# One list of places for all jobs, with the engine of each written down, in a planned attention and mixer kernel

## The chip, the cores and the metric

The kernel runs on one core of a Trainium2 chip. A core has TensorE (matmuls), VectorE, ScalarE, GpSimd (POOL in the rows), and SyncE, which here only issues DMAs. The metric is device time in microseconds (us) of one execution.

## The reference

Causal attention over 4 batches, 12 heads, 448 positions of width 64, then a mixer on the result `x` (448 x 768 in each batch), all in float32:

```python
scores = scale * np.matmul(q, k.transpose(0, 1, 3, 2))
scores = np.where(mask, -1000000000.0, scores)
attn = softmax(scores)                  # row maximum taken off, sum + 1e-09
x = np.matmul(attn, v)                  # heads side by side: 448 x 768
h = np.maximum(x.transpose(0, 2, 1) @ w_tok1, 0.0) @ w_tok2    # over positions
u = x + h.transpose(0, 2, 1)
out = u + np.maximum(u @ w_ch1, 0.0) @ w_ch2                   # over channels, 768 -> 1536 -> 768
```

(`softmax` stands for four lines of the reference.)

## The kernel before, in words

The heads are taken in pairs, 24 of them (`g`), six to a batch. For a pair: `load_pair` brings q, k and v; `prep` turns q and k on VectorE; `heads` does the scores on TensorE (`qk`, line 888, in two halves), takes row bounds on VectorE (`low`, line 910), exponentials with row sums on ScalarE (`expo`, line 922), then a small addition (`guard`, line 941) and a reciprocal (line 944). The probabilities are scaled (`norm`, through `copy`, lines 550 and 552) and transposed: the first ten pairs on TensorE (`by_tensor`, `flip`, line 979), the others by a transposing DMA on 16-bit halves (`by_dma`: `split`, DMA at line 1031, `merge`, through `words`, lines 556 and 558). `values` multiplies the result, the tile `pt`, with v (line 1075). `xturn` turns the result (line 1114) and splits it into a high and a low part, as every matmul of the mixer is done in three products of such parts. `tokens` does the two products over positions (lines 1162 and 1195), `split_u` splits the sum, `channels` and `group` do the products over channels (lines 1245, 1573, 1644, 1664), with weights that `narrow` and `parts` prepare: load, three steps on ScalarE and VectorE, a high part (`wh`) and the difference (`wl`, through `minus`, line 561). `store` and `finish` send the output. The weights of `tokens` have their own splits, in `token_weights` (`w1hi`, `w1lo`, `w2hi`, `w2lo`).

None of this is issued at once. Each step calls `plan.job`, with a planned cost for each engine that can do it, the jobs it needs, the buffers it holds and a rank. There are 2,335 jobs. `Plan.emit` then keeps a clock of its own and, whenever an engine is free on it, gives that engine the job of lowest rank among those whose needs are met and whose buffers are open. What it gives is the order of the program; an engine runs its instructions in that order. The rank of a job is that of its group (2.0 times the pair, and so on) plus a number from the table `NUDGE`, which has one number for all jobs of the same function and rank. Where several engines can do a job, the table `ONLY` names one for some groups, and for the rest a rule in `emit` decides (`BIAS`, `FIRST`, `EARLY`): the engine that takes the job must be the one that would end it first, with a handicap for each engine.

Where TensorE has no job on the planner's clock in the first 75 us and has been busy too little, `emit` issues `keep_warm` (line 778): a matmul of the mask tile by itself, 512 columns, whose result nobody reads.

Of the kernel before, what the change touches and what calls it, by code (L numbers as in the profile page):

```python
# [20 lines left out]
NUDGE = {  # L21
    "load_pair.blocks": {-2: -5.69, 0: -0.18, 2: 9.42, 4: 34.85, 6: 51.99, 8: 70.18, 10: 68.38, 12: -63.34,
        14: 307.44, 16: -211.48, 18: 1.58, 22: 59.15, 24: -9.93, 28: 0.02, 30: 485.43, 32: -30.92, 34: 1.04, 36: 2.18,
        38: -113.03, 40: 409.72, 42: 100.41, 44: -29.88},
    "load_pair.load": {0.5: 20.36, 2.5: -53.93, 4.5: 9.42, 6.5: 0.88, 8.5: 242.83, 10.5: 16.05, 12.5: 0.11,
        14.5: -63.34, 16.5: 0.03, 18.5: 31.27, 22.5: 29.43, 24.5: 16.6, 26.5: 117.07, 28.5: 0.11, 32.5: -0.55,
        34.5: 1.07, 38.5: 13.95, 40.5: 4.04, 42.5: -1.86, 44.5: 180.84, 46.5: -102.76},
    "load_pair.lower": {-0.2: -2.64, 3.8: -10.26, 5.8: -2.41, 7.8: 21.12, 9.8: 1.62, 13.8: 9.47, 15.8: -35.82,
        21.8: 29.43, 23.8: -9.31, 25.8: -12.47, 27.8: 0.13, 29.8: 31.38, 31.8: 31.04, 35.8: 27.32, 37.8: -7.85,
        39.8: 51.43, 41.8: -25.4, 45.8: 20.31},  # L30
    "load_pair.upper": {-0.2: -2.4, 1.8: 7.04, 3.8: 6.92, 5.8: -38.06, 9.8: -135.49, 11.8: -8.1, 13.8: -1.57,
        15.8: -37.81, 17.8: 12.16, 23.8: -89.08, 25.8: -67.22, 27.8: -3.95, 29.8: 7.11, 31.8: -0.97, 33.8: -6.33,
        37.8: -50.92, 39.8: -13.98, 41.8: 35.44, 43.8: 184.58, 45.8: 60.49},
    "narrow.load": {3.5: 36.16, 12: 184.21, 13: -0.75, 15: 1.63, 16: -155.64, 17: 80.6, 18: 1.18, 19: -3.98,
        21: -25.25, 22: -31.03, 23: 2.89, 24: -71.56, 25: -147.25, 27: 5.6, 28: -7.93, 29: -30.33, 30: -32.57,
        31: -0.15, 32: 17.21, 33: 66.76, 34: 41.75, 35: -91.73},
    "narrow.size": {3.5: -95.77, 13: -3.03, 14: 0.59, 15: 1.63, 17: 0.9, 18: -1.77, 19: -30.27, 21: -0.59, 22: 0.06,
        23: -32.71, 25: 30.04, 26: 14.77, 27: 6.97, 29: -25.08, 30: 0.04, 31: 69.05, 32: 0.35, 33: -0.72, 34: -12.68,
        35: -18.38},
    "narrow.shift": {3.5: -39.08, 12: -45.95, 13: -22.05, 14: 51.06, 15: -37.08, 16: 8.91, 17: 34.81, 18: 52.69,  # L40
        19: 16.31, 20: 19.85, 21: 6.15, 22: 148.69, 23: -16.03, 24: -33.15, 26: 110.05, 28: -6.86, 30: -0.29,
        31: -28.04, 32: -56.71, 33: 6.39, 34: -92.95, 35: 76.44},
    "narrow.join": {3.5: -34.13, 12: 72.73, 13: -67.18, 15: -0.22, 16: -15.64, 17: -42.91, 18: 337.03, 19: -32.99,
        20: -3.33, 21: -11.67, 22: -21.87, 23: 28.98, 24: -52.27, 25: -37.11, 26: -0.11, 28: 4.53, 30: -55.02,
        31: -18.66, 32: -38.67, 33: 0.07, 34: 172.82, 35: 92.85},
    "token_weights.<lambda>": {3.5: -7.44},
    "token_weights.rest_of": {3.5: 7.83},
    "prep.turn": {-1.5: 17.65, 2.5: -24.12, 4.5: 0.1, 6.5: -10.13, 8.5: -2.4, 12.5: -0.74, 14.5: 16.4, 18.5: 25.24,
        20.5: 64.35, 22.5: 76.68, 24.5: 54.69, 26.5: 13.64, 28.5: 13.68, 30.5: 5.63, 32.5: 1.14, 34.5: 19.37,
        36.5: 8.97, 38.5: -1.03, 40.5: 35.56, 42.5: 123.8, 44.5: -119.2},  # L50
    "heads.<lambda>": {0: -24.44, 2: -159.72, 4: -0.05, 6: 113.65, 8: 3.12, 10: 0.97, 12: 354.23, 14: -142.06,
        16: -43.97, 18: 52.02, 20: 87.45, 22: 61.7, 24: 12.81, 26: 1.2, 30: -2.24, 32: 122.48, 34: 141.23, 36: -10.17,
        38: 0.02, 40: 8.83, 42: -10.82, 44: 156.23},
    "heads.low": {0: 0.25, 2: 41.64, 6: -286.14, 8: -4.08, 10: -8.1, 12: 223.68, 14: 1016.35, 16: 767.17, 18: 134.37,
        20: 36.56, 24: 259.08, 26: -101.41, 28: 14.92, 30: 4.79, 34: 2.07, 36: 6.95, 38: -3.49, 40: 1.25, 42: -10.4,
        44: -155.06, 46: 25.76},
    "heads.expo": {0: 0.69, 2: 65.52, 4: 78.63, 6: 39.16, 8: 11.37, 10: 455.98, 12: 396.16, 14: -45.41, 16: -8.34,
        18: 134.37, 20: -16.55, 22: -10.41, 24: 203.57, 26: -86.73, 30: 12.87, 34: 2.07, 36: -25.22, 38: 1.67,
        40: -10.67, 42: 12.66, 44: -308.91, 46: 24.15},
    "heads.guard": {0: -45.33, 2: 1.89, 4: 10.39, 6: 0.51, 8: 33.2, 10: 499.55, 12: 379.6, 14: -1.91, 16: -8.27,  # L60
        18: -41.43, 20: -1.85, 22: -232.88, 24: -21.38, 26: -116.5, 28: 84.38, 34: -6.15, 36: 79.09, 38: 1.21,
        40: -0.86, 42: 9.74, 44: -41.52, 46: 9.28},
    "heads.recip": {0: 11.8, 4: 16.05, 6: 18.33, 8: -79.14, 10: -2.88, 12: 43.13, 16: -63.95, 18: -3.79, 20: -19,
        22: -0.44, 24: 164.82, 28: 36.75, 30: -0.68, 32: -4.73, 34: -3.56, 36: -1.87, 38: 75.88, 40: -0.8, 42: 6.81,
        44: 127.73, 46: 0.03},
    "by_tensor.norm": {0: 17.18, 2: 24.16, 6: 2.65, 8: -0.78, 10: -1.93, 12: -3.78, 14: -73.1, 18: 9.56},
    "values.pv": {0: 44.92, 2: -73.62, 6: -11.44, 8: -61.4, 10: -47.37, 12: -12.03, 14: 21.32, 16: -82.88,
        18: -106.29, 20: 59.59, 24: 4.27, 28: -0.09, 30: 0.7, 34: 0.08, 36: -43.42, 38: -13.99, 40: -1.77, 42: -4.13,
# [12 lines left out]
        41: -12.64, 43: -0.55, 45: -4.69},
    "by_tensor.flip": {2: 22.46, 4: -94.38, 6: -48.95, 8: -0.63, 10: 4.97, 12: -6.6, 14: 375.47, 16: -40.39, 18: 10},
    "xturn.twice": {1: -40.45, 5: -61.16, 9: 14.26, 17: 25.81, 21: 1.6, 25: -6.91, 29: 87.65, 33: 1.12, 37: 1.51,
        41: 68.8, 45: 1.15},
    "xturn.none": {1: -35.52, 5: -149.33, 9: -0.41, 13: 0.01, 17: 0.32, 21: -12.3, 25: 67.43, 29: -23.48, 33: -127.73,
        37: -16.01, 45: 11.99},
    "tokens.tok1": {4.5: -2.49, 8.5: 13.1, 12.5: 0.42, 16.5: -32.58, 20.5: -1.53, 24.5: -5.35, 32.5: -45.94,
        36.5: 7.23, 40.5: -1.94, 48.5: -18.08},
    "tokens.relu": {-5: -496.54},
    "tokens.lo": {-5: 26.43},  # L90
    "tokens.tok2": {4.5: 3.06, 8.5: -7.61, 12.5: 15.8, 16.5: 14.51, 20.5: -2.1, 24.5: -94.87, 28.5: -76.06,
        32.5: 562.97, 36.5: 0.62, 40.5: 1421.86, 48.5: 71.6},
# [66 lines left out]
    "finish.plus": {-6: 210.3},  # L159
    "finish.turn": {-6: -5.28},  # L160
    "finish.evac": {-6: -32.31},
    "finish.send": {-6: 0.08},
}


# [100 lines left out]
class Plan:  # L266
# [6 lines left out]
    SHARE = 0.0  # L273
# [1503 lines left out]
```

## Time and profile before

| | us |
|---|---|
| median of 3 runs | 556.01 (553.76 to 556.63) |
| the profiled execution | 554.26 |
| its span, first to last instruction | 552.5 |
| TensorE busy | 542.3 (98%) |
| VectorE busy | 438.0 (79%) |
| ScalarE busy | 338.8 (61%) |
| GpSimd busy | 123.3 (22%) |

The profile gives for each engine how long it ran instructions, and for each idle time what ended it. A busy TensorE is not one at its peak, since its matmuls overlap: a product of 448 columns is listed with some 366 ns, and six in a row take 1.22 us. PEclk is the share of the clock that was granted. All rows come from the profiled execution.

### The profile page before, as it was taken

How to read it: one execution, taken by the hardware profiler on the slowest of the kernel's cores; microseconds unless marked ns; L12 is line 12 of the kernel's file. 1: busy time of each engine (PE TensorE's matmuls, PEld its weight loads, DVE VectorE, ACT ScalarE, POOL GpSimd, SP SyncE). 2: the span in 40 equal slices, each digit the busy share in tenths (PEclk: the TensorE clock that was granted, in tenths of full speed). 3: DMA queues.
4: the chain of work that ended last, by engine and by line, in shares of the span. 5: the costliest groups of instructions: out<-in, count | busy, mean ns of one | idle time of the engine just before them, and what ended most of it. 6: DMA issues, size and time to landing. Idle time of an engine off the chain costs nothing.

```text
span 552.5 us, 11198 instructions
## 1 busy us (share of the span) xinstructions
PE 542.3 (98%) x3922; PEld 469.7 (85%) x3928; DVE 438.0 (79%) x1062; ACT 338.8 (61%) x780; POOL 123.3 (22%) x182
## 2 busy tenths in 40 slices
PE   8999999998999999999999999999999999999997
PEld 4678788886888988888888788899999999999996
DVE  5898888889897788698787887779998857584854
ACT  4989878898857995696796897663332313140401
POOL 2534461362235001030200210223100313100000
PEclk9999999999999999999999999999999999999999
DMA  6677766898998989989998957328551111111257
GB/s 113 155 153 153 168 153 183 195 185 118 204 211 191 171 191 225 193 152 221 190 190 152 208 149 150 95 84 167 117 122 57 58 57 59 57 58 57 58 71 130
DMA packets 231784, 77.69 MB, mean 141 GB/s; under 512 B 206000, under 2 KB 221232, under 8 KB 231728
## 3 DMA queue, kind: packets, MB, share of 16 engines
q1 hardware_dynamic: 220112, 75.37, 63.9%
q10 hardware_dynamic: 11616, 1.61, 1.8%
q8 instruction: 31, 0.51, 0.4%
q14 instruction: 25, 0.20, 0.2%
HBM read 49.15 MB, written 14.94 MB: 116 GB/s over the span
## 4 chain that ended last, share of the span: by engine, by line
PE 90%; DVE 3%; DMA 2%; SPq 2%; ACT 1%; issue 1%; ACTq 0%; POOL 0%; DVEq 0%
PE ps L1245 30%; PE ps L1664 15%; PE ps L1573 12%; PE ps L1075 7%; PE ps L888 7%; PE ps L1195 5%; PE ps L1162 5%; PE ps L979 3%; PE ps L1644 3%; PE ps L1114 2%; PE ps L778 1%; DMA wraw<-in_moe_w_ch_dram 1%; DMA out_dram<-kq 1%; SPq L806 1%; DVE pt L558 1%
## 5 line engine op out<-in xcount | busy, mean ns | idle before, releaser
L1312 DVE TENSOR_TENSOR u<-ps,u 128x448 f32<-128x448 f32 x118 | 72.7, 620 | 40.0 <-PE ps L1664 27.0
L922 ACT ACTIVATE prob<-prob,stat 128x256 f32<-128x256 f32 (+6 forms) x168 | 83.8, 501 | 20.2 <-DVE stat L910 19.4
L910 DVE CUSTOM_DVE_ANT_0 prob<-ps,mask 128x448 f32<-128x448 f32 (+6 forms) x168 | 63.8, 415 | 5.4 <-PE ps L888 5.1
L1245 PE MATMUL ps<-uh,wh 128*128 128x448 f32 x144 | 55.0, 382 | 0.0
L1245 PE MATMUL ps<-gh,wh 128*128 128x448 f32 x144 | 54.0, 375 | 0.0
L1245 PE MATMUL ps<-uh,wl 128*128 128x448 f32 x144 | 52.9, 367 | 0.2 <-DVE wl L561 0.2
L1245 PE MATMUL ps<-gh,wl 128*128 128x448 f32 x144 | 52.7, 366 | 0.0
L1245 PE MATMUL ps<-gl,wh 128*128 128x448 f32 x144 | 52.7, 366 | 0.0
L1245 PE MATMUL ps<-ul,wh 128*128 128x448 f32 x144 | 52.6, 365 | 0.0
L550 ACT ACTIVATE wh<-wf 128x768 fp32r<-128x768 f32 x32 | 26.8, 842 | 38.5 <-PE ps L1664 21.9
L888 PE MATMUL ps<-kq,kq 64*64 64x128 f32 (+5 forms) x768 | 46.6, 362 | 1.0 <-DVE stat L944 0.6
L552 POOL TENSOR_SCALAR prob<-prob,stat 128x64 f32<-128x64 f32 (+6 forms) x63 | 34.6, 565 | 44.0 <-DVE stat L944 39.1
L888 PEld LDWEIGHTS ps<-kq,kq 64*64 64x64 f32 x768 | 27.9, 132 | 19.3 <-issue 12.9
L556 ACT COPY prob<-prob 128x1024 uint16<-128x1024 uint16 (+1 forms) x45 | 41.5, 941 | 3.3 <-DVE prob L552 2.7
L1075 PE MATMUL ps<-pt,vraw 128*64 128x256 f32 (+2 forms) x480 | 39.7, 310 | 2.8 <-DVE pt L558 2.8
L1075 PEld LDWEIGHTS ps<-pt,vraw 128*64 128x64 f32 x480 | 29.0, 136 | 15.4 <-DVE pt L558 3.2
L561 DVE TENSOR_TENSOR wl<-wf,wh 128x768 fp32r<-128x768 f32 x36 | 35.7, 998 | 2.3 <-ACT wh L550 1.5
L556 ACT COPY pt<-pt 128x384 uint16<-128x384 uint16 (+3 forms) x42 | 33.5, 868 | 4.1 <-PE ps L888 3.0
L550 ACT ACTIVATE u<-wf 128x768 fp32r<-128x768 f32 (+1 forms) x17 | 12.7, 749 | 34.2 <-PE ps L1573 19.5
L922 ACT ACTIVATION_READ_ACCUMULATOR prob<-prob,stat 128x1 f32 x168 | 31.9, 190 | 0.0
L1664 PE MATMUL ps<-u,wh 128*128 128x448 f32 x108 | 30.7, 366 | 0.0
L1245 PEld LDWEIGHTS ps<-uh,wl 128*128 128x128 f32 x144 | 27.0, 188 | 3.2 <-DVE wl L561 1.0
(213 smaller groups left out, 1412.2 us busy)
## 6 DMA issues: line engine op xcount, KB each, us to landing
wraw<-in_moe_w_ch_dram SPq DMA_DIRECT2D x24, 768.0 KB, 5.6
wf<-scratch SPq DMA_DIRECT2D x30, 384.0 KB, 3.4
scratch<-wf SPq DMA_DIRECT2D x24, 384.0 KB, 3.4
vraw<-in_v_dram SPq DMA_DIRECT2D x48, 96.0 KB, 2.7
kq<-in_k_dram SPq DMA_DIRECT2D x60, 56.0 KB, 3.9
kq<-in_q_dram SPq DMA_DIRECT2D x56, 56.0 KB, 2.4
gh<-in_k_dram SPq DMA_DIRECT2D x36, 56.0 KB, 2.5
gl<-in_q_dram SPq DMA_DIRECT2D x36, 56.0 KB, 2.4
```

What stands on the lines that cost most here:

```text
L550: nc.scalar.activation(dst, src, AF.Copy, scale=scale)
L552: eng[e].tensor_scalar(dst, src, scale, 0.0, op0=ALU.mult, op1=ALU.add)
L556: nc.scalar.copy(out, in_)
L561: eng[e].tensor_tensor(dst, a, b, op=ALU.subtract)
L888: nc.tensor.matmul(scores[n].tile[lanes, to:at], lhsT=qe.tile[LANES[j], c * QC:(c + 1) * QC], rhs=ke.tile[LANES[j], slice(*keys)], start=T ...
L910: nc.vector.tensor_tensor_reduce(out=part(c, r), in0=ps.tile[:, at:at + wide(c)], in1=mask[:, S - QC:S + P] if c == 2 else mask[:, S - wid ...
L922: nc.scalar.activation(part(c, r), part(c, r), AF.Exp, bias=stat.tile[:, 0, AT[c]:AT[c] + 1], scale=-1.0, accum_out=stat.tile[:, 1, AT[c]: ...
L1075: nc.tensor.matmul(ps.tile[LANES[j], c * QC:(c + nq) * QC], lhsT=s.tile[:, kb, j] if kb < NCH else ends.tile[:, kb - NCH, j], rhs=view[:, ...
L1245: nc.tensor.matmul(ps.tile[:, :S], lhsT=x.tile[:, at_:at_ + P], rhs=y, start=(n == 0 and i == 0), stop=(n + 1 == w[2] and i == 2),)
L1312: eng[e].tensor_tensor(u, ps.tile[:, :S], u, op=ALU.add)
L1573: nc.tensor.matmul(ps.tile[:, :S], lhsT=l()[:, t * P:(t + 1) * P], rhs=r, start=(t == 0 and n == 0), stop=(t == half - 1 and n == 2),)
L1664: nc.tensor.matmul(ps.tile[:, :S], lhsT=l.tile[:, t * P:(t + 1) * P], rhs=r.tile, start=(n == 0), stop=(n == 3 * len(fs) - 1),)
```

## The change

`NUDGE` and `ONLY` go, and with them the rule that chose an engine. `PLACES` has a number from 0 to 2,334 for each job by itself (a tuple for each function and old rank, in the order in which the jobs are made), and `CHOICE` has a letter for each job that more than one engine can do: a for ScalarE, d for VectorE, p for GpSimd. The old rank is only the key into both. `emit` is otherwise as it was: needs, buffers, its clock and the warming matmuls. Two smaller edits come with it: in `QUARTERS` the two last pairs of score matmuls change places, and the planned costs of the two halves of the scores are new.

```diff
-NUDGE = {
-    "load_pair.blocks": {-2: -5.69, 0: -0.18, 2: 9.42, 4: 34.85, 6: 51.99, 8: 70.18, 10: 68.38, 12: -63.34,
...
+PLACES = {
+    "load_pair.blocks": {-2: (2, 3), 0: (4, 5), 2: (20, 10), 4: (52, 70), 6: (138, 160), 8: (213, 238), 10: (272,
...
-ONLY = {
-    "token_weights.<lambda>": {3.5: "act"},
-    "token_weights.rest_of": {3.5: "pool"},
...
+CHOICE = {
+    "token_weights.<lambda>": {3.5: "pppppppp"},
+    "token_weights.rest_of": {3.5: "ddppddpp"},
...
-    BIAS = {"act": 600.0, "dve": 4500.0, "pool": 6850.0}
-    FIRST = {"act": 425.0, "dve": 1000.0, "pool": 500.0}
-    EARLY = 50.0
-    SHARE = 0.0
...
-        only = ONLY.get(name, {}).get(round(rank, 3))
-        if only in costs:
+        key = name, round(rank, 3)
+        nth = self.seen[key] = self.seen.get(key, -1) + 1
+        if len(costs) > 1:
+            only = {"a": "act", "d": "dve", "p": "pool"}[CHOICE[name][key[1]][nth]]
             costs = {only: costs[only]}
-        rank = rank + NUDGE.get(name, {}).get(round(rank, 3), 0.0)
+        rank = PLACES[name][key[1]][nth]
...
-                    if open_ and len(j.costs) > 1:
-                        bias = self.BIAS if j.rank >= self.EARLY or j.rank < -4 else self.FIRST
-                        end = until(j, e, now) + bias[e]
-                        open_ = all(
-                            end <= until(j, o, max(free[o], now)) + self.SHARE * load[o] + bias[o]
-                            for o in j.costs if o != e
-                        )
...
-                (0, 2, 4), (1, 2, 4), (0, 3, 3), (1, 3, 3), (0, 3, 1), (1, 3, 1), (0, 2, 2), (1, 2, 2))
+                (0, 2, 4), (1, 2, 4), (0, 3, 3), (1, 3, 3), (0, 2, 2), (1, 2, 2), (0, 3, 1), (1, 3, 1))
...
-        for rg, cost in zip(RG, (825.0, 695.0)):
+        for rg, cost in zip(RG, (820.0, 850.0)):
```

Line numbers of the changed kernel are 83 higher from the planner's middle on (line 550 is 633, line 778 is 861, line 1114 is 1197, line 1162 is 1245).

What the lists do to the program is seen in the order of each engine's instructions. TensorE before, from the value products of the third pair to the second of eight warming matmuls that stand ahead of a transpose (`vend` is the end of v, `u` the result of the attention, `prob` the probabilities):

```order
144 L1075 MATMUL ps_529<-pt_424,vend_98 64x64 x6
145 L778 LDWEIGHTS mask
146 L778 MATMUL ps_87<-mask 128x512
...
149 L1114 MATMUL ps_577<-ident,u_369 128x128 x4
150 L778 LDWEIGHTS mask
151 L778 MATMUL ps_87<-mask 128x512
```

TensorE now, from the value products of the same pair to the first product over positions:

```order
144 L1158 MATMUL ps_551<-pt_450,vend_98 64x64 x6
145 L1062 MATMUL ps_593<-across_ident,prob_1_94 128x128 x4
146 L971 MATMUL ps_603<-kq_546,kq_588 64x448 x2
147 L971 MATMUL ps_604<-kq_546,kq_588 64x384 x2
...
155 L971 MATMUL ps_617<-kq_546,kq_588 64x128 x2
156 L1197 MATMUL ps_641<-ident,u_393 128x128 x4
157 L1062 MATMUL ps_650<-ident,prob_1_95 128x128 x3
158 L861 LDWEIGHTS mask
159 L861 MATMUL ps_87<-mask 128x512
160 L1245 MATMUL ps_659<-xh_478,w1hi 128x256
```

The scores of the fifth pair now stand where warming matmuls stood; one warming matmul is left there.

ScalarE before, around the first splits of the token weights (`stat` holds row sums, `wf` a weight before it is split):

```order
40 L610 ACTIVATE wf_492<-wl_418 128x256
41 L939 ACTIVATE stat_449<-stat_449 128x3
42 L550 ACTIVATE u_369<-ps_451 128x448
43 L550 ACTIVATE w1hi<-wf_474 128x256
44 L550 ACTIVATE w1hi<-wf_492 128x256
45 L610 ACTIVATE wf_535<-wh_435 128x256
46 L550 ACTIVATE xh_394<-ps_523 128x4x128
47 L922 ACTIVATE prob_1_94,stat_449<-prob_1_94,stat_449 128x320
```

ScalarE now, at the same place:

```order
44 L693 ACTIVATE wf_510<-wl_435 128x256
45 L1005 ACTIVATE prob_1_94,stat_423<-prob_1_94,stat_423 128x320
46 L1005 ACTIVATE prob_1_94,stat_423<-prob_1_94,stat_423 128x192
47 L633 ACTIVATE u_393<-ps_469 128x448
48 L1022 ACTIVATE stat_423<-stat_423 128x4
49 L633 ACTIVATE pt_450<-ps_516 128x3x128
50 L693 ACTIVATE wf_540<-wh_443 128x256
51 L633 ACTIVATE pt_549<-ps_528 128x4x128
```

The writes of `w1hi` are gone from ScalarE; GpSimd has them, among the scalings of the same pairs:

```order
37 L635 TENSOR_SCALAR w1hi<-wf_474 128x256
38 L635 TENSOR_SCALAR w1hi<-wf_510 128x256
39 L635 TENSOR_SCALAR prob_1_95<-prob_1_95,stat_423 128x256
40 L635 TENSOR_SCALAR w1hi<-wf_540 128x256
41 L644 TENSOR_TENSOR w1lo<-wf_540,w1hi 128x256
```

In ScalarE's queue the evacuations into `pt` follow in their place.

## Rows read from the trace of the kernel before

**Rows 1.** Top of the page: busy us, share of the span, instructions.

```profile
span 552.5 us, 11198 instructions
PE 542.3 (98%) x3922; PEld 469.7 (85%) x3928; DVE 438.0 (79%) x1062; ACT 338.8 (61%) x780; POOL 123.3 (22%) x182
```

**Rows 2.** Busy us by stretch; columns in the first line.

```profile
core 0: us, PE busy (x) PEld busy (x) DVE busy (x) ACT busy (x) POOL busy (x), PEclk, DMA share, GB/s
0.00:20.00 20.00, 17.40 (x175) 10.15 (x177) 13.20 (x60) 11.98 (x38) 7.01 (x26) 1.00 0.63 108
20.00:40.00 20.00, 19.58 (x193) 14.30 (x195) 17.48 (x53) 17.77 (x58) 9.99 (x20) 1.00 0.76 175
40.00:60.00 20.00, 19.84 (x216) 16.09 (x210) 18.27 (x59) 19.30 (x57) 8.11 (x14) 1.00 0.76 152
60.00:345.00 285.00, 281.92 (x2310) 241.72 (x2312) 234.75 (x645) 226.83 (x526) 71.57 (x105) 1.00 0.87 182
345.00:540.00 195.00, 195.00 (x996) 180.15 (x995) 149.03 (x237) 61.46 (x101) 26.62 (x18) 1.00 0.33 80
540.00:553.00 13.00, 8.56 (x45) 7.30 (x43) 5.23 (x11) 1.43 (x4) 0.00 (x0) 0.90 0.74 133
```

**Rows 3.** TensorE's waits: us in total, times, longest.

```profile
PE ps L1075 <- DVE pt L558: 2.8, 2, 2.0
```

**Rows 4.** Chain of waits, 21 to 47 us: start, us, what.

```profile
21.46 1.51 PE ps L778 x7
...
33.05 1.73 PE ps L778 x8
...
43.44 2.67 PE ps L1195 x12
```

**Rows 5.** Chain of waits, 25 to 33 us.

```profile
25.43 0.76 ACT prob L922 x2
...
28.38 0.32 ACT w1hi L550
...
31.79 0.55 ACT u L550
...
32.39 0.66 PE ps L1114 x4
```

**Rows 6.** Groups of instructions: busy us, mean ns of one, idle before.

```profile
L550 ACT ACTIVATE w2hi<-wf 128x224 fp32r<-128x224 f32 x4 | 1.6, 394 | 0.5 <-DVE wf L620 0.5
L550 ACT ACTIVATE w1hi<-wf 128x256 fp32r<-128x256 f32 x4 | 1.5, 408 | 0.0
...
L561 POOL TENSOR_TENSOR wl<-wf,wh 128x768 fp32r<-128x768 f32 x6 | 11.6, 1940 | 0.4
...
L561 DVE TENSOR_TENSOR wl<-wf,wh 128x768 fp32r<-128x768 f32 x36 | 35.7, 998 | 2.3 <-ACT wh L550 1.5 <-POOL wh L552 0.5
```

**Rows 7.** Chain of waits, 352 to 362 us.

```profile
352.70 1.92 PE ps L1075 x32
354.62 1.43 PE ps L1245 x6
...
358.92 1.32 PE ps L1162 x11
360.24 1.22 PE ps L1245 x6
```

**Rows 8.** Chain of waits, 298 to 308 us.

```profile
298.74 5.35 DMA wraw<-in_moe_w_ch_dram
...
306.37 0.83 DVE wf L620
307.20 0.52 DVE pt L558
```

**Rows 9.** Line 941 (ns min/median/max), then GpSimd and VectorE at 130 us.

```profile
L941 DVE TENSOR_SCALAR stat<-stat x20: 153/162/994, 68.5 to 339.9; 128x3 f32<-128x3 f32 x10, 128x4 f32<-128x4 f32 x10
...
130.27 1.14 POOL L561 TENSOR_TENSOR ul<-u,uh 128x448 fp32r<-128x448 f32 x1 [0.25 <-ACT uh L550]
...
130.44 0.99 DVE L941 TENSOR_SCALAR stat<-stat 128x3 f32<-128x3 f32 x1
```

More of the change, by code (lines that the diff above doesn't have):

```diff
@@ new lines @@
+CHOICE = {
[6 rows of a table added]
+    "token_weights.<lambda>": {3.5: "pppppppp"},
+    "token_weights.rest_of": {3.5: "ddppddpp"},
+    "heads.guard": {0: "pp", 2: "da", 4: "pd", 6: "pa", 8: "ap", 10: "dp", 12: "pp", 14: "pp", 16: "dp", 18: "ad",
+        20: "ap", 22: "pp", 24: "da", 26: "dd", 28: "pp", 30: "pd", 32: "ad", 34: "ap", 36: "ap", 38: "ad", 40:
+        "da", 42: "pd", 44: "dd", 46: "pa"},
+    "by_tensor.norm": {0: "ddadppp", 2: "padpppa", 4: "ppdpppa", 6: "dppadpa", 8: "papppap", 10: "appadpa", 12:
+        "ppppaad", 14: "appapap", 16: "pppdpdp", 18: "dpadada"},
+    "by_tensor.evac": {0: "adda", 2: "aaaa", 4: "adda", 6: "adaa", 8: "aaaa", 10: "aaad", 12: "aada", 14: "adaa",
+        16: "daad", 18: "adaa"},
+    "values.evac": {0: "d", 2: "a", 4: "a", 6: "a", 8: "a", 10: "a", 12: "d", 14: "a", 16: "a", 18: "a", 20: "d",
+        22: "a", 24: "a", 26: "d", 28: "a", 30: "a", 32: "d", 34: "d", 36: "d", 38: "a", 40: "d", 42: "a", 44: "a",
+        46: "a"},
+    "xturn.<lambda>": {-1: "a", 1: "a", 3: "a", 5: "a", 7: "d", 9: "a", 11: "a", 13: "a", 15: "a", 17: "a", 19: "a",
+        21: "a", 23: "d", 25: "a", 27: "d", 29: "a", 31: "a", 33: "d", 35: "a", 37: "a", 39: "a", 41: "a", 43: "d",
+        45: "d"},
+    "xturn.twice": {1: "a", 5: "p", 9: "p", 13: "p", 17: "p", 21: "a", 25: "a", 29: "p", 33: "a", 37: "a", 41: "a",
+        45: "a"},
+    "xturn.none": {1: "a", 5: "p", 9: "p", 13: "p", 17: "a", 21: "p", 25: "p", 29: "p", 33: "p", 37: "p", 41: "a",
+        45: "p"},
+    "split_u.hi": {12.5: "daaaaa", 24.5: "aaadda", 36.5: "aaddaa", 48.5: "daaaaa"},
+    "split_u.lo": {12.5: "dppppd", 24.5: "ppdppd", 36.5: "dppppd", 48.5: "pppppp"},
+    "by_dma.norm": {20: "ddaapap", 22: "ddppaad", 24: "aaadppa", 26: "appapap", 28: "apadaap", 30: "aadadda", 32:
+        "ppaaaad", 34: "pdaappd", 36: "aaddpaa", 38: "apdaddd", 40: "pddddpa", 42: "ppapppp", 44: "ddpapaa", 46:
+        "pppaapd"},
+    "by_dma.split": {20: "aaad", 22: "adaa", 24: "dadd", 26: "ddaa", 28: "dddd", 30: "adda", 32: "daaa", 34: "adaa",
+        36: "adda", 38: "addd", 40: "aaad", 42: "adda", 44: "aadd", 46: "ddaa"},
+    "by_dma.merge": {20: "daad", 22: "aaad", 24: "daaa", 26: "adda", 28: "aada", 30: "adaa", 32: "addd", 34: "adad",
+        36: "ddad", 38: "aadd", 40: "aaad", 42: "adda", 44: "adda", 46: "ddaa"},
+    "mixtures.mix.lo": {48.6: "ppddddpddpdp"},
[3 rows of a table added]
+        -4.92: "adap", -4.91: "adap", -4.9: "adad"},
+    "combined.split.lo": {-4.94: "dddd", -4.93: "dpdd", -4.92: "dppd", -4.91: "dpdp", -4.9: "dpdd"},
+    "spared.lo": {-4.9: "dd"},
+    "finish.evac": {-6: "aaad"},
@@ L286, in __init__ @@
         self.filler = None
+        self.seen = {}
     def warm(self, now):
@@ L351, in emit @@
         left = len(self.jobs)
-        load = dict.fromkeys(self.ENGINES, 0.0)
         def offer(j):
-            if len(j.costs) == 1:
-                for e in j.costs:
-                    load[e] += j.costs[e]
             for e in j.costs:
@@ L403, in emit @@
                 pick.done = True
-                if len(pick.costs) == 1:
-                    load[e] -= pick.costs[e]
                 for s in pick.takes:
```

261 lines of the change are left out of this document (118 added, 143 removed), and 138 rows, old and new, of tables (CHOICE, NUDGE, PLACES).

## The prediction

> **What bounds the kernel now.** I read the busy times first, then the same by stretch, then TensorE's waits, then the chain of waits around the places where TensorE does not do work of the reference. TensorE is busy 542.3 of 552.5 us; no other engine is above 79% [rows 1]. By stretch it is full from 60 us on, with small holes; in 540 to 553 us TensorE is busy 8.56 of 13, which is the drain of the last stores and is fixed [rows 2]. So the order of the other engines counts only where TensorE waits for one of them, or where the planner has put a warming matmul (line 778, it multiplies the mask by itself) because nothing was free.
>
> Waits are few: two on VectorE's `pt` copies, 2.8 us together [rows 3]. Warming matmuls are more: the order of before has 57 (the profile recorded 51). Seven of them take 1.51 us and eight 1.73 [rows 4], so 0.216 us each and 12.3 us in all. The chain shows why those around 33 us stand there: from 25.4 to 32.3 us it runs almost only through ScalarE, which then lets line 1114 start, and the next thing TensorE has is eight warming matmuls [rows 4, 5]. ScalarE is busy 17.77 of 20 us in 20 to 40 and 19.30 of 20 in 40 to 60 [rows 2]: there it sets the pace as much as TensorE.
>
> **The change part by part.** The sum is made against the profiled execution's 554.26 us (span 552.5 and 1.8 around it), which is 0.3% under the median 556.01. The matmuls of the reference are the same, one for one, so TensorE's useful work is unchanged. What changes is read from the order of the instructions.
>
> Warming matmuls: 57 become 37. Up to the third pair's scores there are 29 for 28; between there and the first token product 7 for 22; from the second token block on 1 for 7. At 0.216 us each the 20 are 4.3 us. They are a gain only where the work that follows them can start earlier. What stood in the way between 21 and 36 us was ScalarE [rows 5], and the new list takes the eight splits of the token weights (`w1hi`, `w2hi`) from it: four at 0.408 and four at 0.394 us [rows 6], 3.2 us. GpSimd does them; it was busy 9.99 of the 20 us there [rows 2]. Against that stands that more pairs of the attention are asked for in the same time: ahead of the first second-layer token product there are twelve score blocks instead of ten, with their exponentials on ScalarE. I let one fifth of the 4.3 us come back as short waits and take -3.4. Ends: -4.3, and 0 if all come back; what is late next is then ScalarE's evacuation of transposes into `pt`.
>
> Changes of tile shape: scores and value products use 64-wide tiles, the rest 128. In TensorE's order there are 88 such changes before and 78 now. Six channel matmuls right behind a value product take 1.43 us, six that follow a token product 1.22 [rows 7]: 0.2 us for each of five round trips, -1.0. Ends: 0 and -2.0, if entering costs as much as leaving.
>
> The two named waits on `pt`: at 306 us the merge of `pt` stood in VectorE's queue behind the join of a weight (line 620) whose DMA took 5.35 us [rows 8]. Every one of VectorE's places is new, so this very wait need not come again, and others like it can. I leave 2.8 us of such waits in the forecast. Ends: -2.8, and +4, two more of the size of the longest (2.0).
>
> Engines written down: 331 of the 2,335 jobs run elsewhere. ScalarE has 16 instructions fewer, VectorE 10 fewer, GpSimd 26 more. Seven of GpSimd's are differences of 128x768 at 1.94 us, where VectorE took 0.998 [rows 6]; the other 19 at its mean of 123.3/182 = 0.68 us make 13, together 26.5 us more on an engine at 22% [rows 1]. Off TensorE's path unless a product waits for such a weight, so 0 there. The indirect price is the port.
>
> A row that speaks against it: the guard of a row sum on VectorE takes 0.162 us in the median and once 0.994, and that once begins at 130.44 while GpSimd is in a difference from 130.27 to 131.41 [rows 9]. It ended with it. So 0.8 us were lost on VectorE, in front of the `pt` copies for which TensorE waited longest [rows 3]. The Trainium skill, SBUF — State Buffer, section "Who interferes with whom", states it as a rule: VectorE's 2-port modes and GpSimd share one pair of ports, and whoever comes second is blocked for the whole instruction. By that rule, and the row agrees, each of the 26 instructions can cost VectorE up to its own length. What it would give is a rival below.
>
> The narrow score matmuls (`QUARTERS`): the last two pairs change places, with the same tiles and columns. The second half of the scores lasted 0.98 us before; no row shows it the other way round. I take 0, since the tiles that can run side by side are the same pairs; a tenth of 0.98 either way in 24 pairs is 2.4 us either way.
>
> The longer price of scores in the planner (820 and 850 ns for 825 and 695) only moves the planner's clock; on the chip it costs nothing itself, and its effect is in the counts above. The late stage, 345 to 540 us, has TensorE full in every microsecond [rows 2]; its product order changes, its length cannot. There are nine more channel-down blocks behind the last value product (15 for 6), so attention ends earlier against the products; that is order, not time.
>
> Sum: -3.4 - 1.0 = -4.4 us, 549.9 us on the profile's scale. A median stands 0.3% above that; half of it belongs to the runs shown, so I say 550.5 us. The forecast's own range is 548 to 553.
>
> **The rivals.** First, waits in place of warming matmuls: ScalarE at 19.30 of 20 us [rows 2] cannot go much faster, so TensorE stands idle where it was warming; then only the tile changes remain, 554.26 - 1.0, about 554.5 on the median's scale. For it: rows 2; against it: the 3.2 us taken from ScalarE.
>
> Second, slower: VectorE is blocked by GpSimd. Place: 60 to 345 us, where `pt` merges, norms and word splits, all in the fast form, stand between scores and value products. Price: if half of the 26.5 us fall on such instructions, VectorE is 13 us later in a stretch where it is 82% busy (234.75 of 285 us [rows 2]); less 10 instructions at its mean of 438.0/1062 = 0.41 us [rows 1], 9 us. It decides from the point where VectorE has no reserve left, and the wait of 2.0 us [rows 3] shows that there are such points; there each microsecond passes to TensorE. 550.5 + 9 gives about 559.5.
>
> Third, all goes through: no warming matmul comes back (-0.9 more) and both waits on `pt` vanish (-2.8): 546.8.
>
> Fourth, the clock. Granted clock was full speed, 2.4 GHz, in every stretch up to 540 us, and 0.90 in the mean only at the end, where TensorE was busy 8.56 of 13 us [rows 2]. With 20 warming matmuls gone, idle stretches before 45 us may let it fall to 1.2 GHz; five microseconds of work at half speed cost up to 5 and bring 555.5. The Trainium skill, TensorE: Matmul & The Clock Gate, "HAM oscillation", warns of just that for kernels whose TensorE waits between bursts; no stretch before 540 us shows it here. Last, that the list does not do what it says: the counts above are from the built order, so I give that nothing.
>
> **How the numbers follow.** Forecast (548 to 553) 0.46; waits instead of warming (553 to 556.5) 0.22; blocked VectorE 0.11; all goes through (545 to 548) 0.16; clock 0.05. A measurement of this kernel tells about 0.5% from no change: 553.2 and 558.8 are the bounds. Faster: 0.46 + 0.16 and a little of the second, 0.64. Slower: most of the blocked case and a little of the clock's and of the unknown, 0.12. Same: 0.24. The range, 546 to 556, leaves out the blocked case and the outer half of the best one; the likeliest one's own is 548 to 553.
>
> **What would show it.** Right: about 37 matmuls of the mask line, one at most behind 45 us; TensorE's busy time near 538 us with a span near 548; the first second-layer token product no later than 44 us although two more score blocks stand ahead of it (it started at 43.44 [rows 4]); no wait of TensorE on ScalarE above 1 us. The tile term: six channel matmuls behind a value product still near 1.43. Wrong: TensorE waiting 3 us or more in the first 70 us for `pt` or `stat`; guards and `pt` copies on VectorE near 1 us while GpSimd runs; a granted clock below full in any stretch before 540 us; or new waits in 100 to 340 us of more than 6 us together.

## The result, and the profile after

| | before | after |
|---|---|---|
| median | 556.01 us (553.76 to 557.14) | 550.76 us (550.39 to 551.25) |
| ratio to before | | 0.9908, 95% interval 0.9884 to 0.9933 |
| span of the profiled execution | 552.5 us | 548.6 us |

The time came out where I had put it (550.5). The steps that led there did not all hold. The page of after begins, in answer to [rows 1]:

```profile
span 548.6 us, 11162 instructions
PE 538.4 (98%) x3908; PEld 466.3 (85%) x3908; DVE 432.7 (79%) x1052; ACT 325.0 (59%) x764; POOL 151.0 (28%) x208
```

TensorE works 3.9 us less and the span is 3.9 us shorter; GpSimd works 27.7 us more (I had said 26.5). By stretch, beside [rows 2]:

```profile
0.00:20.00 20.00, 17.58 (x164) 9.54 (x166) 14.05 (x59) 12.92 (x44) 7.78 (x26) 1.00 0.66 110
20.00:40.00 20.00, 19.91 (x241) 15.21 (x237) 17.25 (x65) 17.33 (x55) 8.41 (x19) 1.00 0.73 167
40.00:60.00 20.00, 18.04 (x199) 14.99 (x199) 18.06 (x62) 18.96 (x61) 12.28 (x22) 1.00 0.75 140
60.00:345.00 285.00, 283.66 (x2340) 244.15 (x2335) 240.56 (x638) 220.85 (x519) 92.53 (x123) 1.00 0.87 185
345.00:540.00 195.00, 195.00 (x960) 179.12 (x959) 140.29 (x226) 53.92 (x85) 30.00 (x19) 1.00 0.34 79
```

In 40 to 60 us TensorE now has a hole of 2 us; in 60 to 345 it has 1.7 us more work than before. The warming matmuls (line 861), and TensorE's waits in answer to [rows 3]:

```profile
L861 PE MATMUL ps<-mask x37: 379/379/634, 1.5 to 45.7; 128*128 128x512 bf16 x37
```

```profile
PE ps L1062 <- POOL prob L635: 2.8, 2, 2.0
PE ps L861 <- POOL mask L654: 1.5, 1, 1.5
PE ps L971 <- DVE kq L938: 0.9, 2, 0.7
PE ps L1328 <- DVE wl L644: 0.5, 1, 0.5
```

There are 37, the last at 45.7 us, as the order said. The two waits on VectorE's `pt` are gone; waits of the same sum are there on GpSimd's norms (`prob`). The chain of waits (start, us, what) shows the longer of them:

```profile
38.90 1.88 DMA gl<-in_q_dram
40.78 0.19 DVE w2lo L644
...
41.07 0.38 DVE wf L703
41.45 0.09 DVE stat L1027
...
41.89 0.65 POOL prob L635
...
42.59 0.66 PE ps L1062 x4
...
46.09 1.01 PE ps L1278 x5
```

A reciprocal of 0.09 us stood on VectorE behind two steps of a token weight, the norm on GpSimd behind the reciprocal, and TensorE behind the norm. The first second-layer token product begins at 46.09, not by 44 as I had asked.

**Where the 3.9 us are.** I laid TensorE's records block by block (a block is one planned piece of its work) beside the same list, gave each kind of block the duration that it has where nothing delays it (the lower third of before's and after's), and added up what each execution took beyond that, warming matmuls, waits and tile changes alike. The columns are stretches of equal work done; 60 us of work are done at some 81 us of the run, 100 at 123, 150 at 176, 300 at 330, 500 at 532. "Own" is that execution's time, "median" that of its kernel's runs.

```
lag in us         to 60  60-100  100-150  150-200  200-350  350-500  end | own     median
before             21.3    1.9      4.3      1.1      4.9      0.1   4.2 | 554.26  556.01
after              19.7    1.9      2.2      1.6      2.4      1.5   4.6 | 550.4   550.76
before_no_fill     21.6    1.9      4.3      1.1      4.7      0.1   5.2 | 555.42  556.11
before_pt_first    22.0    1.9      6.6      1.1      3.8      0.1   4.2 | 556.2   556.77
after_fill_back    21.0    3.7      1.4      4.1      2.9      1.5   4.8 | 555.82  552.89
after_no_warm      18.6    3.4      1.4      3.6      2.4      1.5   4.0 | 551.45  550.66
after_token_act    18.9    1.9      1.4      1.6      2.4      1.5   4.9 | 549.14  549.42
after_moves        17.7    1.9      2.1      4.6      2.4      1.5   5.1 | 551.82  548.99
after_best         17.2    2.6      1.4      3.7      2.4      1.5   4.6 | 549.79  549.52
new_then_old       19.5    3.5      5.9      1.1      3.9      1.1   4.3 | 555.57  552.97
old_then_new       21.6    4.1      1.5      1.7      2.9      0.1   5.0 | 553.20  553.42
```

After is 1.6 us ahead at 60 us of work, 3.7 at 150, 5.7 at 350, and then gives 1.8 back, 1.4 of it in the late stage. (Where two kernels do the same, their stretches agree to 0.1 us, as 1.9 or 1.5 here; so small differences can be read.)

The 3.9 us are those of two executions; the medians differ by 5.3. A part of this lies in the clock of single runs. Of the 60 runs of before that were timed beside the experiments, the 41 with a mean granted clock of 0.998 or more have a median of 553.83 us, the 19 with 0.997 or less 555.88. All five runs of after had 0.998 or more. In the two profiled executions the clock was full to 540 us, so the table does not hold this part; experiment 6 shows where it can arise.

### The profile page after: what moved, and what is told of

Its sections match the earlier page's. It is cut to its first block, busy times and chain, and to the rows that moved or that the text cites. A ratio compares the mean times of both kernels' runs of the same rounds, so it can differ in the third digit from the quotient of the medians.

```text
span 548.6 us, 11162 instructions
## 1 busy us (share of the span) xinstructions
PE 538.4 (98%) x3908; PEld 466.3 (85%) x3908; DVE 432.7 (79%) x1052; ACT 325.0 (59%) x764; POOL 151.0 (28%) x208
## 4 chain that ended last, share of the span: by engine, by line
PE 86%; DMA 6%; SPq 4%; DVE 1%; issue 1%; ACT 1%; POOL 0%; ACTq 0%; DVEq 0%
PE ps L1328 31%; PE ps L1747 14%; PE ps L1656 12%; PE ps L1158 6%; PE ps L971 6%; PE ps L1278 5%; PE ps L1245 4%; PE ps L1727 3%; SPq L889 3%; PE ps L1062 2%; DMA out_dram<-kq 2%; DMA vraw<-in_v_dram 2%; PE ps L1197 2%; DMA gl<-in_q_dram 1%; DMA wl<-in_moe_w_tok_dram 1%
## 5 line engine op out<-in xcount | busy, mean ns | idle before, releaser
L1005 ACT ACTIVATE prob<-prob,stat 128x128 f32<-128x128 f32 (+6 forms) x168 | 83.6, 500 | 17.5 <-DVE stat L993 17.3
L993 DVE CUSTOM_DVE_ANT_0 prob<-ps,mask 128x256 f32<-128x256 f32 (+6 forms) x168 | 63.5, 416 | 7.5 <-PE ps L971 7.1
L633 ACT ACTIVATE wh<-wf 128x768 fp32r<-128x768 f32 x28 | 23.3, 842 | 52.4 <-PE ps L1747 33.1
L635 POOL TENSOR_SCALAR prob<-prob,stat 128x320 f32<-128x320 f32 (+6 forms) x70 | 38.2, 556 | 56.6 <-DVE stat L1027 42.9
L644 POOL TENSOR_TENSOR wl<-wf,wh 128x768 fp32r<-128x768 f32 x17 | 32.6, 1917 | 59.4 <-ACT wh L633 57.5
L971 PE MATMUL ps<-kq,kq 64*64 64x64 f32 (+5 forms) x768 | 45.4, 360 | 0.9 <-DVE kq L938 0.9
L971 PEld LDWEIGHTS ps<-kq,kq 64*64 64x64 f32 x768 | 26.0, 132 | 19.7 <-issue 12.3
L639 ACT COPY pt<-pt 128x512 uint16<-128x512 uint16 (+3 forms) x45 | 38.7, 907 | 1.2 <-DMA pt<-prob 1.0
L633 ACT ACTIVATE prob<-prob,stat 128x320 f32<-128x320 f32 (+6 forms) x58 | 28.1, 510 | 2.9 <-DVE stat L1027 2.8
L1328 PEld LDWEIGHTS ps<-uh,wh 128*128 128x128 f32 x144 | 27.1, 188 | 2.7 <-issue 0.5
```

The source lines that it names most:

```text
L633: nc.scalar.activation(dst, src, AF.Copy, scale=scale)
L635: eng[e].tensor_scalar(dst, src, scale, 0.0, op0=ALU.mult, op1=ALU.add)
L639: nc.scalar.copy(out, in_)
L644: eng[e].tensor_tensor(dst, a, b, op=ALU.subtract)
L971: nc.tensor.matmul(scores[n].tile[lanes, to:at], lhsT=qe.tile[LANES[j], c * QC:(c + 1) * QC], rhs=ke.tile[LANES[j], slice(*keys)], start=T ...
L993: nc.vector.tensor_tensor_reduce(out=part(c, r), in0=ps.tile[:, at:at + wide(c)], in1=mask[:, S - QC:S + P] if c == 2 else mask[:, S - wid ...
```

## The experiments

In all of them the planner makes its list of (engine, job) as it was, and the list is edited before the instructions are issued, if nothing else is said. Each was timed against before on the same chip; ratios are to before.

**1. before_no_fill.**

```diff
+    late = set(fills[28:])
+    return [x for i, x in enumerate(order) if i not in late]
```

> The kernel before, in its own order and with its own engines, without the 29 warming matmuls that stand behind the third pair's scores; the planner's clock still counts them, so nothing else moves. My theory (a warming matmul there stands in for a wait, and the gain came from the work behind it being released earlier by the new order): TensorE then waits where it warmed, at most 1.5 us are won, ratio to before 0.997 to 1.000, waits of about 5 us on ScalarE and VectorE appear in the profile. Rival A (each is TensorE time and nothing else): 29 x 0.216 = 6.3 us are won, ratio 0.989. Rival B (they hold the clock): the granted clock falls below full between 20 and 50 us and the time rises, ratio 1.003 or more.

1.0031 (1.0014 to 1.0047). Its page and its waits:

```profile
PE 539.3 (97%) x3897; PEld 466.9 (84%) x3899; DVE 438.0 (79%) x1062; ACT 339.7 (61%) x780; POOL 123.5 (22%) x182
```

```profile
PE ps L1091 <- DVE pt L574: 3.0, 2, 2.0
PE ps L1130 <- ACT u L566: 1.5, 3, 0.6
...
PE ps L995 <- POOL prob L568: 1.3, 2, 1.0
```

TensorE's busy time fell nearly to that of after and the time did not: where it warmed it waits now, for `u`, for norms. In before these matmuls cost nothing. Rival A fell. My own range (up to 1.000) was missed by a little: in the trace 1.0 of the 1.2 us is in the drain at the end. Rival B is not settled: in the profiled execution the granted clock stayed at 1.00 in every stretch to 540 us, but 7 of the 9 runs had a mean granted clock of 0.995 to 0.997, against 5 of the 20 of before beside them, and no trace tells where it fell in those.

**2. after_fill_back.**

```diff
+MORE = {30: 4, 33: 9, 36: 4, 37: 3}
+            out += [(e, j)] * MORE.get(fills, 0)
```

> The kernel after, with 20 warming matmuls put back at four of the places where it still has some between 20 and 46 us (4, 9, 4 and 3 more), so that it has 57 as before; the order of all else is untouched. My theory (behind these places work is ready, TensorE's time is the bound): 4.3 us are added, less up to 2.0 that vanish from the wait on GpSimd's norm at 40.6 us: 2.3 to 4.3 us, ratio to before 0.995 to 0.9985. Rival A (TensorE's time, all of it): 0.9985. Rival B (the matmuls only cover waits): no change, ratio 0.991.

0.9982 (0.9963 to 1.0): by the ratios 4.1 us more than after, with more than 1 us of uncertainty on either side. In after, TensorE has work behind these places. But of the profiled execution's lag (555.82 us, the longest of twelve; median 552.89) only 1.3 us more than in after are there by 60 us of work; the rest are waits later on, 1.4 us for `u` and 0.7 for a weight. So the sum fits "20 x 0.216" without the trace showing it spent there.

**3. after_token_act.**

```diff
+    return [("act" if ... j.key[0] == "token_weights.<lambda>" else e, j) for e, j in order]
```

> The kernel after, with only the eight splits of the token weights put back from GpSimd to ScalarE, in the same places of the emission order. My theory (ScalarE in the way, 8 x 0.40 = 3.2 us): 1.5 to 3 us slower than after, ratio to before 0.9935 to 0.996. Rival A (the new wait of 2.0 us on GpSimd's norm at 40.6 us stands behind such a split in GpSimd's queue, and goes away): 1 to 2 us faster than after, ratio 0.987 to 0.989. Rival B (neither matters): 0.991.

0.9918 (0.9899 to 0.9937), the same as after: rival B. By stretch and by waits:

```profile
20.00:40.00 20.00, 19.57 (x235) 15.13 (x236) 17.11 (x64) 19.25 (x63) 6.32 (x13) 1.00 0.77 170
```

```profile
PE ps L1070 <- POOL prob L643: 1.5, 1, 1.5
```

ScalarE is busy 19.25 of 20 us, more than the 17.77 of before [rows 2], and TensorE does not mind. The wait on GpSimd's norms fell from 2.8 to 1.5 us, as rival A had it, without a gain clear of the noise. The relief of ScalarE, on which my largest term stood, is not what made the early part quicker.

**4 and 5. after_old_engines and after_choice_old.** The first gives each of the 331 jobs its old engine at the moment of issue; in the second `CHOICE` itself has the old letters and the planner plans with them.

```diff
-    "token_weights.<lambda>": {3.5: "pppppppp"},
+    "token_weights.<lambda>": {3.5: "aaaaaaaa"},
...
```

> The kernel after in its own emission order, with the 331 jobs given to the engines that had them before; the planner's clock does not know it, so the order, the 37 warming matmuls and the 78 tile changes stay. My theory (of the engines only the eight token-weight splits count, the rest is worth 0): ScalarE is 3.2 us later near 30 to 42 us, about 2 us come back as waits there, ratio to before 0.994 to 0.996. Rival A (the order alone makes the gain): 0.990 to 0.992. Rival B (an order and its engines fit each other, and any others make waits all along): over 1.000.

> The list of places as after has it, but with the engine that each of the 331 jobs had before, and planned so: the planner knows, keeps engine queues in step, and lays 53 warming matmuls and 100 tile changes instead of 37 and 78. Theory A (a list holds only with the engines it was made for; the two cannot be told apart as terms of a sum): slower than before, ratio 1.003 to 1.02, with small waits all along 100 to 340 us. Theory B (the order is what counts and the planner repairs the rest): 0.991 to 0.996. From the counts alone (16 warming matmuls as cover at 0, 11 round trips at 0.2) it would be 0.995.

1.0399 (1.0376 to 1.0423) and 1.0315 (1.0285 to 1.0344). TensorE's waits in the second:

```profile
PE ps L1307 <- POOL wl L623: 3.6, 3, 1.2
PE ps L1307 <- DVE wl L623: 2.4, 3, 1.6
PE ps L1307 <- ACT wh L612: 2.3, 1, 2.3
PE ps L1635 <- DVE pt L623: 2.3, 2, 1.3
```

The new places with the old engines are 17 to 22 us slower than before. There is no term "engines" that could be 0: the new places need the new engines. (The old places with the new engines were not run.) My expectation for the first was wrong, rival B and theory A right.

**6. before_pt_first.**

```diff
+    (("by_dma.merge", 22.0, 0), ("heads.low", 24.0, 4)),      # four of this pair
+    (("by_dma.merge", 40.0, 2), ("narrow.shift", 33.0, 0)),   # two of this one
```

> The kernel before with six merges of pt moved forward in VectorE's queue: the four of one pair ahead of three exponent steps, a copy and an add (near 132 us), two of another ahead of the weight step that waited for a load (near 305 us). Nothing else moves. Theory A (these two waits, 2.0 and 0.8 us and their restarts, are real terms that a new order of VectorE can simply win, and the list won them): 2.5 to 3.2 us faster than before, ratio 0.994 to 0.9955. Theory B (my forecast: waits of that size come back elsewhere on VectorE): ratio 0.999 to 1.001.

1.0034 (1.0018 to 1.0049). The two waits went and others came:

```profile
PE ps L1139 <- DVE u L577: 2.0, 2, 1.8
PE ps L803 <- POOL mask L596: 1.5, 1, 1.5
PE ps L1139 <- ACT u L575: 0.8, 1, 0.8
```

In the table the second move wins 1.1 us (200 to 350: 3.8 for 4.9), the first loses 2.3 (100 to 150: 6.6 for 4.3). The evacuation of `u` that the merges overtook is the next thing that TensorE needs, so the wait of 2.0 us on `pt` became one of 1.8 on `u`, and another of 0.8 on `u` came behind it. The larger part of the loss in this execution is the clock: behind the 1.8 us it was at 1.2 GHz from 136.7 to 140.2 us (last but two number, 0.59 in the mean of these 4 us), and the value products there took 2.75 us, where they took 1.64 in before (the second fence; the third is before):

```profile
136.00:140.00 4.00, 4.00 (x40) 3.10 (x43) 1.70 (x5) 3.83 (x10) 0.00 (x0) 0.59 0.42 84
```

```profile
136.41 2.75 PE L1100 MATMUL ps<-pt,vraw 128*64 128x256 f32 x20
```

```profile
135.80 1.64 PE L1075 MATMUL ps<-pt,vraw 128*64 128x256 f32 x20 [1.98 <-DVE pt L558]
```

Block by block the fall costs some 1.6 of the 2.3 us. It is not the whole loss of this kernel: its three runs with a mean granted clock of 0.998 or more took 555.61 to 556.77 us, such runs of before beside them 553.89 in the median. So a wait of this kind can be won, but not by moving one step ahead of another that is as urgent; and a wait of 2 us can cost more than its length.

**7 and 8. after_moves and after_best.** Eight jobs forward; after_best also leaves out the last eight warming matmuls.

```diff
+    (("heads.guard", 8.0, 0), ("narrow.size", 3.5, 6)),
+    (("heads.recip", 8.0, 0), ("narrow.shift", 3.5, 6)),
+    (("heads.recip", 12.0, 0), ("prep.turn", 14.5, 1)),
+    (("parts.<lambda>", 18.0, 1), ("load_pair.lower", 23.8, 0)),
...
```

> The kernel after with eight jobs moved forward in three places where TensorE waits now: the guard, reciprocal and two norms of one pair ahead of token-weight steps (near 40 us), two reciprocals ahead of a transpose that waits for its load (near 63 us), one weight difference ahead of a copy that waits for its load (near 129 us), and one evacuation ahead of an exponent. Theory A (what is left in after are short steps queued behind a step that waits for a DMA or another engine): the waits of 2.0, 0.8 and 0.5 us go, 2.5 to 3.7 us faster than after, ratio to before 0.984 to 0.986. Theory B (TensorE then waits for the next thing, scores behind a late load): under 1 us, 0.989 to 0.991.

> The kernel after with the eight forward moves of the earlier run and without its last eight warming matmuls (behind the third pair's scores). Theory A (early waits and warming matmuls are time, and add up): 1.7 us more than the moves alone, 3 to 4 us faster than after, ratio to before 0.984 to 0.987. Theory B (what is won before 100 us comes back between 150 and 200 us, as the moves alone did by their profile): as after, 0.989 to 0.992.

0.9906 (0.9881 to 0.9932) and 0.9909 (0.9884 to 0.9934): as after, theory B both times. It is not that the moves did nothing: after_best is 2.5 us ahead of after at 60 us of work and 2.6 at 150. At 200 it has 0.6 left. The chain of waits of after_best shows where that is paid:

```profile
167.33 5.88 DMA wraw<-in_moe_w_ch_dram
...
173.31 0.90 ACT wf L719
...
175.42 0.88 DVE wf L729
...
176.45 0.85 POOL wh L661
...
177.37 1.83 POOL wl L670
```

```profile
PE ps L1354 <- POOL wl L670: 1.2, 1, 1.2
```

A weight is loaded, taken apart in four steps, and TensorE waits 1.2 us for the last. Its split and its difference are two of the 331 jobs: before had them on ScalarE and VectorE, where such a difference takes 0.998 us [rows 6], not 1.83. The transfers are busy there with or without the moves; 170 to 190 us of after and of after_best (TensorE's busy time first, the last but one number the DMA share):

```profile
170.00:190.00 20.00, 20.00 (x192) 16.19 (x191) 17.27 (x55) 15.83 (x37) 4.17 (x5) 1.00 1.07 186
```

```profile
170.00:190.00 20.00, 18.62 (x184) 14.59 (x177) 15.37 (x52) 15.89 (x37) 4.54 (x5) 1.00 1.11 195
```

That TensorE waits here because it came early is not shown, and two runs speak against it: after_fill_back comes to 150 us of work 2.3 us behind after and loses 4.1 us up to 200, after_token_act comes 1.6 us ahead and loses 1.6, as after does. What goes with the loss is a load. Of the three loads of weights issued from 149 to 183 us the slowest took 5.2 us from issue to landing in after, and 7.3 in after_best:

```profile
DMA to landing us min/median/max: 4.5/5.2/5.2
```

```profile
DMA to landing us min/median/max: 4.7/5.9/7.3
```

It took 7.3, 7.3 and 7.2 us in after_moves, after_no_warm and after_fill_back too, which lose 3.6 to 4.6 us there, and 5.2 and 5.5 in after_token_act and old_then_new, which lose 1.6 and 1.7. Why it lands later in the first group is open. The weight's difference back on VectorE would be the next thing to try; it was not tried. No kernel here beats after by more than its interval.

**9. after_more_changes.**

```diff
+        if s[1].tiled and t[1].tiled and near:      # two neighbours with 64-wide tiles
+            order.remove(y)                         # y: the next channel block
+            order.insert(order.index(t), y)
```

> The kernel after with 23 channel blocks pulled in between two neighbouring blocks of scores or value products on TensorE: 23 more round trips between the 64-wide and the 128-wide tiles, the same matmuls. Theory A (my term, 0.2 us for each round trip): 4.6 us slower than after, ratio to before 0.999. Rival (leaving a narrow block is dear, entering it free, as little as 0.1 each): 2.3 us, 0.995. Rival (the change of tile shape costs nothing, the 0.2 us was a wait): 0.991. Above 1.003 it would be waits made by the moves, to be read in the profile.

1.0254 (1.0226 to 1.0282): far above 1.003, so it is waits for the most part (7.9 us by name for `u`, `xl` and `wl`), and the clock fell once: behind a wait of 1.9 us on `u` it is 0.57 in the mean of 208 to 212 us. The table's method separates what is left. Blocks behind which nothing waited over 0.3 us lose in the mean 0.12 us on entering narrow tiles and 0.06 on leaving them in before (41 and 40 of them), 0.13 and 0.03 in after (37 and 37), 0.15 and 0.06 here (57 and 50). A round trip is 0.16 to 0.21 us; my 0.2 was near enough, though most of it is at the entrance, not where I had read it.

**10. after_no_warm.**

```diff
+    return [x for x in order if x[1].order >= 0]
```

> The kernel after without any of its 37 warming matmuls, the 14 at the very start among them; the order of all else is untouched. Theory A (they are cover only, and TensorE's clock does not need them where it has work): ratio to before 0.989 to 0.992, granted clock full from 20 us on. Theory B (the clock is what they are for): TensorE's granted clock is at 1.2 GHz for some microseconds behind 4 us, each of them costing half of itself, 3 to 8 us slower than after, ratio 0.997 to 1.006.

0.9919 (0.9895 to 0.9943): the same as after. The first 20 us:

```profile
5.00:10.00 5.00, 3.31 (x32) 1.71 (x32) 2.99 (x10) 1.09 (x4) 0.00 (x0) 1.00 0.70 114
10.00:15.00 5.00, 2.70 (x39) 1.79 (x39) 4.96 (x28) 4.77 (x16) 0.46 (x2) 1.00 0.61 112
15.00:20.00 5.00, 4.20 (x39) 2.47 (x39) 3.86 (x15) 4.00 (x18) 3.82 (x8) 0.66 0.66 118
```

Theory B was right about the clock and wrong about the time. With TensorE busy 2.70 of 5 us, the granted clock fell to 0.66 in the mean of the next 5, that is to 1.2 GHz in about two thirds of them; it was full again from 20 us on. At 25 us of work this kernel is within 0.3 us of after (16.8 us of lag for 16.5): by that, what sets the pace so early is not TensorE. The Trainium skill, TensorE: Matmul & The Clock Gate, "HAM oscillation", warns of bursts with waits between them; the trace agrees that the clock falls. A price for it does not show against after; among the six runs the three with a mean granted clock of 0.996 or 0.997 took 550.92 to 551.45 us, the other three 549.63 to 550.39.

**11 and 12. new_then_old and old_then_new.** The list of one kernel for its first 87 (or 90) blocks on TensorE, 82 to 87 us, then the rest of the jobs in the other kernel's order and on its engines. At this seam the two have done the same jobs but for eight.

```diff
-THEN = (rest of after)
+THEN = (rest of before)      # and the mirror image
```

> The emission order, the engines and the warming matmuls of after up to about 82 us of the run (its first 87 blocks of TensorE's work), and from there the order and engines of before for all that is left. Theory A (the gain is made early, by the work that starts sooner behind fewer warming matmuls): nearly all of it, ratio to before 0.991 to 0.993. Theory B (by the profiles: up to that point after is 1.6 us ahead, the rest is won later): 0.996 to 0.998. Theory C (what is won early is given back where loads of weights and scores set the pace, as when I moved eight jobs forward): 0.999 to 1.001.

> The mirror image: before's order, engines and 57 warming matmuls up to about 85 us (90 blocks), then the order and engines of after. Theory A (the gain is made early): 0.999 to 1.001. Theory B (by the profiles after wins 3.7 us between 85 and 345 us and loses 1.4 us behind it): ratio to before 0.994 to 0.9965. Theory C (all of it is won there, the early part is worth nothing): 0.990 to 0.992.

0.9965 (0.9944 to 0.9985) and 0.9994 (0.9973 to 1.0014). The early part alone is worth 1.9 us (0.8 to 3.1), as the lag had it (1.6). (In the profiled execution of new_then_old the wait on `pt` near 134 us is that of before, 1.98 us, but behind it the granted clock fell to 0.57 in the mean of 136 to 140 us; its 100 to 150 us of work lose 5.9 us for 4.3.) The late part alone seemed worth nothing, against my expectation; the table shows why. old_then_new loses 2.2 us more than either parent at 60 to 100, right behind the seam (its largest single loss, 1.9 us, is at 92.6 us, ahead of a value product), and from 100 to 500 it lags 6.2 us, where before lags 10.4 and after 7.7. So by the trace the late order does win its 4 us, and the seam and a somewhat longer drain take most of it; the times alone do not show it.

## Why the prediction came out right

**Warming matmuls (-3.4): count right, price wrong.** 37 of them, TensorE busy 538.4 (I had said about 538). But "at 0.216 us each the 20 are 4.3 us", with one fifth coming back, is the step that failed. Taking 29 out of before won nothing (1.0031), taking all 37 out of after lost nothing (0.9919). The early part did get shorter, by 1.6 us in the trace and 1.9 us in new_then_old, and of the 4.3 us about three quarters came back, as the 2.0 and 0.8 us on GpSimd's norms, 3.2 with the restarts behind them: some -1.1 stands where -3.4 was forecast. The premise behind it, that ScalarE was in the way at 21 to 36 us and the token-weight splits free it, fell with after_token_act. The rest of the early 1.6 us is at tile changes (0.7 less up to 60 us of work). What in the order of the first 87 blocks brings this about is open.

**Tile changes (-1.0): right, somewhat small.** Entering and leaving together cost 7.3 us in before (41 x 0.122 + 40 x 0.058) and 5.9 in after (37 x 0.127 + 37 x 0.033): -1.4. Rows of the sort that I had read are there in after as well, here nine channel matmuls behind a token product (first row) and behind a value product:

```profile
323.31 1.83 PE ps L1328 x9
...
331.20 2.03 PE ps L1328 x9
```

The Trainium skill, TensorEngine Tiling (Array Packing), "Key Properties", says that a change of tiling mode drains TensorE; by that rule each change has a price, and these 0.2 us agree.

**Waits on `pt` (kept at 2.8): mis-sized.** Between 100 and 350 us of work the lag fell from 10.3 to 6.2 us, 4.1 in all, of which the two places of [rows 3] are about 3.2 with the restarts behind them, and tile changes most of the rest. I had let waits of that size come back on VectorE; behind 100 us only one of 0.5 us did (`wl` at 130 us). They came back, but early and on GpSimd, where I had counted them under the warming matmuls.

**Engines (0): not a term.** GpSimd's load was right in sum, not in its parts: there are eleven more differences of 128x768 on it, 17 for 6 [rows 6], where I had counted seven:

```profile
L644 POOL TENSOR_TENSOR wl<-wf,wh 128x768 fp32r<-128x768 f32 x17 | 32.6, 1917 | 59.4 <-ACT wh L633 57.5
```

The load hid as I had said for after itself; but with the old engines the same places are 3 to 4% slower than before, and the sentence "unless a product waits for such a weight" came true at 177 us of after_best.

**The port (rival two): the price fell, the thing itself did not.** With more work on GpSimd no guard of VectorE is above 171 ns, where before had one of 994 [rows 9]. But one of GpSimd's took 1038 ns, from 113.76 us, and ended within 0.1 us of a step of VectorE on a weight (113.77 to 114.72). It did not add up to a slower kernel. Line 1024 of after (ns min/median/max):

```profile
L1024 POOL TENSOR_SCALAR stat<-stat x21: 221/228/1038, 10.1 to 308.0; 128x4 f32<-128x4 f32 x11, 128x3 f32<-128x3 f32 x10
L1024 DVE TENSOR_SCALAR stat<-stat x15: 126/158/171, 15.7 to 293.2; 128x4 f32<-128x4 f32 x8, 128x3 f32<-128x3 f32 x7
```

**Late stage (0): 1.4 us slower,** and 0.4 in the drain; see the last section. **The clock (rival four)** stayed full to 540 us in the two profiled executions, and my sum gave it no part in before. Single runs show that it has one. Behind the wait of 1.98 us on `pt` near 134 us it stayed full in before's profiled execution and fell in that of new_then_old. Of the kernels that have before's order there (before, before_no_fill, before_pt_first, new_then_old) 41 of 93 runs had a mean granted clock of 0.997 or less; of those that have after's order there and its early warming matmuls (after, after_token_act, after_fill_back, after_moves, after_best, old_then_new) 4 of 47. So a part of the measured gain is probably that this wait is gone and the clock falls less often; traces of single executions cannot show how much.

**`QUARTERS` and the planned costs** were not run by themselves. For the first the traces agree with my 0: a second half of the scores takes 0.978 us in the median in before and 0.977 in new_then_old, which has the new pairs. The second stays open.

So -4.4 stood for -1.6 early, -4.1 between 100 and 350, and +1.8 late: -3.9, as the span has it. The gain that I had placed in the warming matmuls was for the greater part in the waits and tile changes from 100 to 350 us of work, and the errors cancelled: that the sum met the time so closely was luck. The cause is shown for the early part by new_then_old; for the part from 100 to 350 us it is read from the traces, since the one run that moved the merges alone won nothing.

## What to carry to other kernels

A matmul that fills idle time is worth nothing until a run without it says so: count it as a wait with another name, and ask what released the work behind it. A gain can be lost again far behind its place, here to a load that landed 2 us later; so follow the lag stage by stage, and look in more than one run before naming the reason. Read the granted clock of single runs as well as the profile's: a wait that costs 2 us in one execution can cost 1.6 more in another. A table of order and a table of engines that were made together are judged together: the new order on the old engines was slower than the old kernel.

## What the runs showed of the hardware

In the late stage the same matmuls of 128 x 448 run at one of two steady paces. From 444 to 522 us of after each begins 206.7 ns behind the last; elsewhere, and in before throughout these stretches, it is some 202.7 ns. Seven matmuls in after and six in before:

```profile
469.64 0.37 PE L1747 MATMUL ps<-h1l,wh 128*128 128x448 f32 x1
...
471.09 0.37 PE L1747 MATMUL ps<-u,wl 128*128 128x448 f32 x1
```

```profile
469.64 0.37 PE L1664 MATMUL ps<-u,wl 128*128 128x448 f32 x1
...
470.86 0.36 PE L1664 MATMUL ps<-u,wl 128*128 128x448 f32 x1
```

That is 1.45 us for 7 and 1.22 for 6, with TensorE called fully busy and its clock full in both. Some 370 matmuls at 4 ns are the 1.5 us of the late stage. It is not the order alone: old_then_new, with the same late order, does not show it (0.1 us), nor does after_old_engines, with after's whole order on other engines (202.7 from 436 to 520 us); new_then_old, with before's late order, shows it from 414 to 440 us (206.7, 1.1 us in the table). What sets the pace was not found.

The granted clock can fall in the middle of a run, and need not do so each time: behind a wait of 1.98 us near 134 us TensorE went on at 2.4 GHz in before and for 3.4 us at 1.2 GHz in new_then_old.
